# State products two at a time, two batches' scores turned by TensorE, four products in plain fp32

## The chip, the cores and the metric

The kernel runs on one core of one Trainium2 chip. The metric is the device time of one execution in microseconds, as the median of several runs. A profiled execution gives the trace from which the rows below are read.

## The reference

Per batch b (8) and head (8), with x of 512 rows, a state of 32 rows and D = 64, two attentions are computed, and their rows go through a two-layer MLP with softplus:

```python
scores = scale * np.matmul(x, state.transpose(0, 1, 3, 2))
a = np.exp(scores - scores.max(-1, keepdims=True))
a /= a.sum(-1, keepdims=True) + 1e-09
xread = np.matmul(a, state)
scores2 = scale * np.matmul(state, x.transpose(0, 1, 3, 2))
a2 = np.exp(scores2 - scores2.max(-1, keepdims=True))
a2 /= a2.sum(-1, keepdims=True) + 1e-09
sread = np.matmul(a2, x)
attn = np.concatenate([xread, sread], axis=2)
# heads side by side: rows of 512
h = rows @ w_in                      # 4608 x 512 x 2048
g = np.maximum(h, 0.0) + np.log1p(np.exp(-np.abs(h)))
out = g @ w_out                      # 4608 x 2048 x 512
```

The weights come in double precision; the output is fp32.

## The kernel before

**The algebra.** xread is not formed. For each batch b and each chunk c of 512 columns of w_in the kernel forms the *state product* V = state @ w_in of each head (`heads`, L308), and the first layer is then h = V^T a, a product over 256 pairs of head and state row instead of 512 model columns. The second half, 256 rows of sread, is carried to the end as "batch 8".

**Precision.** Operands of the big products are split into a high and a low part in fp32r (`split`, L232: a cast `vh`, `ah`, `gh`, `wh` on ScalarE, then a subtraction `vl`, `al`, `gl`, `wl`), and each product runs as three passes (`PASSES`). An MLP product h.b.f (128 of the 2048 columns, 512 rows) is six matmuls of 512 columns, `gemm1` at L468; each of the four m.b.f.c that follow it adds it into one of four accumulators with three matmuls. A state product V.b.c has eight small plain-fp32 products, each of which uses 64 rows and 32 columns of the array (`heads`, L308); it fills two PSUM banks, and the trace shows two instructions for each plain-fp32 product. Scores Q.b have the same form. The read R.b uses 32 columns of the array for each product. G.b.g and T.b are transposes by TensorE (four blocks, and one).

**Softmax of a batch** (`softmax`, L337), for each half g of the heads: A transposes the scores in 32 by 32 blocks on VectorE, M takes the maximum, Ms subtracts, m is the exponential on ScalarE, N the reciprocal sum, Nm multiplies (VectorE or GpSimd), D transposes back into `af`, and ah/al split it. For the sread side, qk copies the scores to SBUF, E and e make the row softmax, G turns it, R multiplies with x, X scales, T turns and th/tl split.

**Weights.** A slice of w_in or w_out is loaded by SP (Li, Lo) and converted by ch (ScalarE), cu and cr (VectorE). The first chunk of w_in comes in four pieces (two halves j of the columns, two halves x of the heads), and the state products of the first chunk of batches 0 and 1 are issued in halves, V.b.0.j.x, as the pieces arrive.

**The order** is written out by hand: `PLAN` is a list of `name:engine:places`, S for SP's loads and stores, T TensorE, V VectorE, A ScalarE, G GpSimd; places are PSUM banks (0 to 7) or SBUF slots. Each engine works through its own entries in that order; an instruction that waits holds up all that stand behind it on its engine. Fillers w.i (two transposes of the identity) stand in TensorE's list where it would have nothing to do at the start. `TURNS` gives the turns in which batches 0 and 1 alternate; from batch 2 on a batch runs from f = 0 to 15.

Of the kernel before, what the change touches and what calls it, by code (L numbers as in the profile page):

```python
# [18 lines left out]
P = 128  # L19
# [9 lines left out]
WARMERS = 60  # L29
PAIRS = ("w8", "o8", "x", "xT", "po", "wf", "W", "V", "a", "g", "u")  # L30

PLAN = """
Lt.0.0:S:0 Lz.0:S:0 Lt.0.1:S:1 Li.0.1:S:2 Lt.1.0:S:3 w.6:T:0 Q.0:T:1,2 Li.0.2:S:4 qk.0.1:A:2 A.0.1:V:1 w.11:T:3 Lz.1:S:3 A.0.0:V:4 ch.0.1:A:5
Lt.1.1:S:5 M.0.1:V: Li.0.0:S:6 qk.0.0:A:6 Lo.1:S:7 cu.0.1:V:8 w.16:T:4 Li.0.3:S:9 M.0.0:V: Ms.0.1:G: w.18:T:5 E.0.0:V: Ms.0.0:G: m.0.1:A: w.21:T:6
e.0.0:A: N.0.1:V: m.0.0:A: G.0.0:T:7 cu.0.2:V:10 ch.0.2:A:7 w.25:T:0 N.0.0:V: Nm.0.1:G: Q.1:T:3,2 D.0.1:V:8 Nm.0.0:G: w.30:T:1 A.1.1:V:9 ch.0.0:A:10
D.0.0:V:11 cr.0.2:V: ah.0.0:A:11 cu.0.0:V: ch.o1:A:12 V.0.0.1.0:T:4,5 M.1.1:V: ah.0.1:A:12 w.39:T:6 cr.0.0:V: Lo.0:S:13 w.40:T:0 ch.0.3:A:13 w.41:T:1
cu.0.3:V: Lo.2:S:14 V.0.0.0.0:T: cr.0.1:V: Lo.5:S:15 w.43:T:6 al.0.0:V: w.44:T:0 V.0.0.0.1:T: al.0.1:V: vh.0.0.0.0:A:16 vh.0.0.1.0:A:17 cr.0.3:V:
vl.0.0.0.0:V: V.0.0.1.1:T: vl.0.0.1.0:V: w.50:T:1 Ms.1.1:V: ch.o0:A:14 Lx.0.0:S:18 h.0.0:T:6 Lx.0.1:S:19 vh.0.0.0.1:A: cu.o0:V:6 m.1.1:A: cu.o1:V:1
Lo.3:S:20 vl.0.0.0.1:V: vh.0.0.1.1:A: h.0.1:T:0 cr.o0:V: ch.o2:A:4 vl.0.0.1.1:V: cr.o1:V: h.0.2:T:1 cu.o2:V:10 A.1.0:V:5 s.0.0:A:7 wh.0:A:21 cr.o2:V:
V.1.0.0.0:T:4,5 gh.0.0:A:22 V.1.0.0.1:T: wl.0:V: s.0.1:A:11 h.0.3:T:6 gl.0.0:V: wh.1:A:23 M.1.0:V: gh.0.1:A:24 m.0.0.1:T:0 wl.1:V: s.0.2:A:8 wh.2:A:25  # L40
V.1.0.1.0:T: gl.0.1:V: gh.0.2:A:26 m.0.0.0:T:1 wl.2:V: s.0.3:A:13 m.0.1.1:T: gl.0.2:V: ga.0.0:A:14 m.0.1.0:T: Ms.1.0:V: gh.0.3:A:27 cu.o3:V:4
qk.1.0:A:12 Li.3.2:S:28 m.0.2.1:T: gl.0.3:V: Lo.6:S:29 m.0.2.0:T: Lo.4:S:30 r.0.0:V: N.1.1:V: Lx.1.0:S:31 m.0.0.2:T:6 m.1.0:A: m.0.1.2:T: E.0.1:V:
# [148 lines left out]
def width(buf):  # L191

    kind = buf.split(".")[0]
    if kind in ("vp", "sc", "gp", "rp", "tp", "h", "acc", "wp"):
        return 0
    return 2 if kind in PAIRS else 1
# [7 lines left out]
def graph(io, at, nc):  # L204
# [89 lines left out]
    W1 = {}  # L294
# [351 lines left out]
```

## Time and profile before

| what | us |
|---|---|
| median of 3 runs (663.84 to 665.02) | 664.52 |
| profiled execution | 664.04 |
| its span | 662.0 |
| TensorE (PE) busy | 650.3 |
| ScalarE (ACT) busy | 341.3 |
| VectorE (DVE) busy | 287.0 |
| GpSimd (POOL) busy | 5.0 |

The span runs from the first to the last recorded instruction of the profiled execution. In a timeline row the first number is the start and the second how long the merged group lasted until its last end; matmuls overlap, so what an item costs on PE is read from its start to the start of the next item. The names say what is written and read: `h<-a,V` is an MLP product, `acc<-W,g` an m product, `vp<-wf,zf` a state product, `sc<-xT,zf` scores, `rp<-x,aT` the read, `gp<-ident,e` a transpose G, `tp` T, `wp` a filler.

### The profile page before, as it was taken

How to read it: one execution, taken by the hardware profiler on the slowest of the kernel's cores; microseconds unless marked ns; L12 is line 12 of the kernel's file. 1: busy time of each engine (PE TensorE's matmuls, PEld its weight loads, DVE VectorE, ACT ScalarE, POOL GpSimd, SP SyncE). 2: the span in 40 equal slices, each digit the busy share in tenths (PEclk: the TensorE clock that was granted, in tenths of full speed). 3: DMA queues.
4: the chain of work that ended last, by engine and by line, in shares of the span. 5: the costliest groups of instructions: out<-in, count | busy, mean ns of one | idle time of the engine just before them, and what ended most of it. 6: DMA issues, size and time to landing. Idle time of an engine off the chain costs nothing.

```text
span 662.0 us, 9405 instructions
## 1 busy us (share of the span) xinstructions
PE 650.3 (98%) x3898; PEld 501.7 (76%) x3898; DVE 287.0 (43%) x540; ACT 341.3 (52%) x583; POOL 5.0 (1%) x10
## 2 busy tenths in 40 slices
PE   6899999999999999999999999999999999999997
PEld 4477777776788878777778777777777788887776
DVE  4898865764542241228212552228213456122220
ACT  3689975754562465337433564337434747243232
POOL 2000000000000000000000000000000000000000
PEclk9899999999999999999999999999999999999999
DMA  8954113300300005000400104000420001000001
GB/s 319 419 200 159 45 51 104 136 1 33 102 26 17 17 32 167 1 33 32 136 1 1 64 6 130 1 33 32 136 64 1 0 2 65 0 21 13 0 1 64
DMA packets 15914, 44.11 MB, mean 67 GB/s; under 512 B 1792, under 2 KB 2816, under 8 KB 15872
## 3 DMA queue, kind: packets, MB, share of 16 engines
q1 hardware_dynamic: 15872, 43.52, 18.8%
q8 instruction: 30, 0.49, 0.3%
q14 instruction: 12, 0.10, 0.0%
HBM read 34.60 MB, written 8.91 MB: 66 GB/s over the span
## 4 chain that ended last, share of the span: by engine, by line
PE 97%; DVE 1%; DMA 1%; ACT 0%; issue 0%; POOL 0%
PE acc L239 56%; PE h L239 30%; PE vp L239 5%; PE sc L239 1%; PE rp L239 1%; PE gp L384 1%; PE h_idle L576 1%; DMA w<-in_w_in_dram 1%; PE wp L446 0%; DVE T L343 0%; DVE wf L286 0%; POOL T L346 0%; PE tp L429 0%; ACT e L373 0%; ACT e L404 0%
## 5 line engine op out<-in xcount | busy, mean ns | idle before, releaser
L239 PE MATMUL acc<-W,g 128*128 128x512 f32 x1632 | 396.7, 392 | 0.0
L239 PEld LDWEIGHTS acc<-W,g 128*128 128x128 f32 x1632 | 303.3, 188 | 75.3 <-issue 11.3
L236 DVE TENSOR_TENSOR g<-t,g 128x512 fp32r<-128x512 f32 x136 | 93.0, 689 | 257.5 <-ACT g L220 257.4
L239 PE MATMUL h<-a,V 128*128 128x512 f32 x768 | 195.5, 394 | 0.0
L453 ACT ACTIVATE t<-h 128x512 f32<-128x512 f32 x136 | 80.7, 599 | 202.6 <-PE h L239 201.9
L239 PEld LDWEIGHTS h<-a,V 128*128 128x128 f32 x768 | 141.9, 188 | 44.4 <-issue 10.1
L220 ACT CAST g<-t 128x512 fp32r<-128x512 f32 x136 | 83.4, 621 | 5.0 <-issue 2.1
L236 DVE TENSOR_TENSOR V<-vp,V 128x512 fp32r<-128x512 f32 (+1 forms) x66 | 42.0, 670 | 46.6 <-ACT V L220 45.7
L220 ACT CAST V<-vp 128x512 fp32r<-128x512 f32 (+1 forms) x66 | 35.2, 577 | 49.3 <-PE vp L239 46.5
L239 PE MATMUL vp<-wf,zf 64*32 64x512 f32 (+1 forms) x544 | 37.8, 582 | 2.8 <-DVE wf L286 1.8
L239 PEld LDWEIGHTS h<-sreadT,u 128*128 128x128 f32 x192 | 24.3, 189 | 1.6 <-issue 0.8
L239 PE MATMUL h<-sreadT,u 128*128 128x256 f32 x192 | 24.7, 284 | 0.0
L453 ACT ACT_TABLE_LOAD x18 | 23.1, 1283 | 1.7 <-PE h L239 1.4
L220 ACT COPY o<-acc 128x512 f32<-128x512 f32 x26 | 14.4, 586 | 10.0 <-PE acc L239 9.4
L239 PEld LDWEIGHTS vp<-wf,zf 64*32 64x32 f32 x544 | 6.8, 105 | 16.0 <-issue 10.7
L343 DVE STREAM_TRANSPOSE T<-sc 128x512 f32<-128x512 f32 x16 | 10.8, 701 | 11.6 <-ACT e L404 10.7
L220 ACT CAST a<-af 128x512 fp32r<-128x512 f32 x16 | 9.8, 622 | 9.9 <-DVE af L357 9.9
L404 ACT COPY e<-sc 128x512 f32<-128x512 f32 x16 | 9.0, 588 | 10.9 <-PE sc L239 10.2
L384 PE MATMUL gp<-ident,e 128*128 128x128 f32 x64 | 9.5, 280 | 4.2 <-ACT e L373 4.2
L220 ACT CAST W<-ow 128x512 fp32r<-128x512 f32 x16 | 10.0, 624 | 6.4 <-PE acc L239 3.5
L350 DVE TENSOR_REDUCE sm<-T 128x16 f32<-128x512 f32 x16 | 10.7, 668 | 5.3 <-ACT T L347 5.3
L236 DVE TENSOR_TENSOR a<-af,a 128x512 fp32r<-128x512 f32 x16 | 10.7, 684 | 5.0 <-ACT a L220 5.0
(61 smaller groups left out, 296.8 us busy)
## 6 DMA issues: line engine op xcount, KB each, us to landing
xT<-in_xt_dram SPq DMA_DIRECT2D x16, 512.0 KB, 5.1
w<-in_w_in_dram SPq DMA_DIRECT2D x16, 512.0 KB, 8.1
o<-in_w_out_dram SPq DMA_DIRECT2D x16, 512.0 KB, 9.4
x<-in_xn_dram SPq DMA_DIRECT2D x16, 512.0 KB, 3.3
out_dram<-o SPq DMA_DIRECT2D x24, 256.0 KB, 2.1
out_dram<-po SPq DMA_DIRECT2D x8, 256.0 KB, 2.7
zf<-in_zp_dram SPq DMA_DIRECT2D x8, 128.0 KB, 5.4
out_dram<-o SPq DMA_DIRECT2D x8, 64.0 KB, 1.7
```

The lines of the kernel that those rows point to most:

```text
L220: nc.scalar.copy(dst, src)
L236: lambda e: eng(e).tensor_tensor(r(dlo()), src(), dhi(), ALU.subtract))
L239: nc.tensor.matmul(dst, lhs, rhs, start=start, stop=stop)
L343: op(f"A.{b}.{g}", "V", tok, [f"{T}:1"], lambda e: nc.vector.transpose(at(T), at(sc)))
L350: nc.vector.tensor_reduce(at(sm), t3(), AX.X, ALU.add)
L384: nc.tensor.transpose(at(f"gp.{b}.{g}")[:, P * c:P * c + P], at(src)[:, P * c:P * c + P], at("ident"))
L404: op(f"qk.{k}", "A", [sc], [f"{ex}:s"], lambda e, sc=sc, ex=ex: nc.scalar.copy(at(ex), at(sc)))
L453: lambda e: nc.scalar.activation(at(f"t.{k}"), at(f"h.{k}"), AF.Softplus))
L576: nc.tensor.matmul(at("h.idle")[:, 0:P], idle, idle, start=True, stop=True)
```

## The change

- **Pairs.** `STATES` lists the state products that are issued together: chunk c of batches 0 and 1 for c = 1 to 3, chunks 0 and 1, and 2 and 3, of each later batch. A pair is sixteen small products in a row, into four PSUM banks. V.1.0 is one full product; V.0.0 keeps its four halves.
- **Scores of batches 0 and 1** (`TURNED`): A and D are transposes by TensorE with the identity, four blocks of 128 by 128 each, into PSUM banks `st` and `ab`; M and Ms read the bank. For batch 0, ac copies the bank to `af`.
- **First four MLP products of batch 0** (h.0.0 to h.0.3): two plain-fp32 products each, from `Vf` (a copy vf of V.0.0) and `af`, in place of six fp32r passes; V.0.0 is not split, and ah.0/al.0 are made later, for the products from f = 4 on.
- **Order and places** are new for the whole table. There are 4 fillers in place of 13. Some copies and conversions have another engine or form (ga on VectorE four times in place of one, cu in its two-step form 13 times in place of 8, ch as Copy 13 times in place of 8, Ms on VectorE always, Nm on GpSimd once in place of twice). The loads at the start come as xT.0 (both), zf.0, xT.1 (both), then w_in pieces 0.0, 0.2, 0.3, zf.1, piece 0.1; before, pieces 0.1, 0.2, 0.0 and 0.3 stood fourth, sixth, ninth and eleventh.

```diff
+TURNED = (0, 1)
+STATES = [((0, c), (1, c)) if c else ((1, 0),) for c in range(4)] + [((b, c), (b, c + 1)) for b in range(2, B) for c in (0, 2)]
...
-vl.0.0.0.0:V: V.0.0.1.1:T: vl.0.0.1.0:V: w.50:T:1 Ms.1.1:V: ch.o0:A:14 Lx.0.0:S:18 h.0.0:T:6 Lx.0.1:S:19 vh.0.0.0.1:A: cu.o0:V:6 m.1.1:A: cu.o1:V:1
+V.1.0:T:5,1 vf.0.0:A: Ms.1.1:V:7 vf.1.0:A: ch.o1:A:9 cr.o0:V: h.0.0:T:2 m.1.1:A: M.1.0:V: wh.0:A:18 N.1.1:V: vh.1.0.0:A:19 h.0.1:T:3 Lo.4:S:20
...
+    for j in range(2):
+        for x in range(2):
+            op(f"V.0.0.{j}.{x}", "T", ["zf.0", W1[0, j, x]], [f"vp.0.0.{g}:{j}{x}" for g in range(2)],
+               lambda e, j=j, x=x: heads(0, 0, (2 * x, 2 * x + 1), slice(256 * j, 256 * j + 256)))
+        for g in range(2):
+            cs = slice(256 * j, 256 * j + 256)
+            op(f"vf.{g}.{j}", "AV", [f"vp.0.0.{g}:{j}{x}" for x in range(2)], [f"Vf.{g}:{j}"],
+               lambda e, g=g, cs=cs: copy(e, at(f"Vf.{g}")[:, cs], at(f"vp.0.0.{g}")[:, cs]))
...
-                op(f"V.{b}.{c}", "T", [f"zf.{b}"] + ins, [f"{v}:" for v in vp], lambda e, b=b, c=c: heads(b, c, range(4), slice(0, 512)))
...
+    for group in STATES:
...
+        def products(e, group=group):
+            for b, c in group:
+                heads(b, c, range(4), slice(0, 512))
+
+        op("V." + "+".join(f"{b}.{c}" for b, c in group), "T", ins, [f"vp.{b}.{c}.{g}:" for b, c in group for g in range(2)], products)
+
+
+    def turned(name, bank, src, tok):
+        def f(e):
+            for c in range(4):
+                nc.tensor.transpose(at(bank)[:, P * c:P * c + P], at(src)[:, P * c:P * c + P], at("ident"))
+
+        op(name, "T", tok, [bank], f)
...
-        op(f"A.{b}.{g}", "V", tok, [f"{T}:1"], lambda e: nc.vector.transpose(at(T), at(sc)))
...
+        if onPE:
+            turned(f"A.{k}", f"st.{k}", ex, [f"{ex}:s"])
+        else:
+            op(f"A.{k}", "V", [sc], [f"{T}:1"], lambda e: nc.vector.transpose(at(T), at(sc)))
+        src, raw = (f"st.{k}", f"st.{k}") if onPE else (T, f"{T}:1")
...
-        op(f"D.{b}.{g}", "V", [f"{T}:4"], [f"af.{b}.{g}"], lambda e: nc.vector.transpose(at(f"af.{b}.{g}"), at(T)))
...
+        if onPE:
+            turned(f"D.{k}", af, T, [f"{T}:4"])
+        else:
+            op(f"D.{k}", "V", [f"{T}:4"], [af], lambda e: nc.vector.transpose(at(af), at(T)))
+        if b == 0:
+            op(f"ac.{k}", "AV", [af], [f"af.{k}"], lambda e: copy(e, at(f"af.{k}"), at(f"ab.{k}")))
+            af = f"af.{k}"
...
-        op(f"e.{b}.{g}", "A", tok + [nm], [out, f"{rs}:1"],
+        op(f"e.{b}.{g}", "A", tok + [nm, f"mx.{b}.{g}"], [out, f"{rs}:1"],
...
+                early = b == 0 and f < 4
...
+                        if early:
+                            mm(at(f"h.{k}"), at(f"Vf.{g}")[:, cs], at(f"af.{b}.{g}"), g == 0, g == 1)
+                        for vi, ai in PASSES if not early else ():
                             mm(at(f"h.{k}"), r(page(f"V.{b}.{f // 4}.{g}", 2, 512)[:, vi, cs]), r(page(f"a.{b}.{g}", 2, S)[:, ai]), n == 0, n == 5)
```

TensorE's list in batch 6, around the state product of its third chunk (`vp_2`; `tp` is T.6, `h_7` the product h.6.7; the second number in `vp_2_0` is the half g), before:

```order
L429 MATMUL tp_4221<-ident,sr_4207 128x128
L239 MATMUL vp_2_0_4223<-wf_0_680,zf_3641 32x512
L239 MATMUL vp_2_1_4224<-wf_0_680,zf_3641 32x512
...
L239 MATMUL vp_2_0_4223<-wf_1_657,zf_3641 32x512
L239 MATMUL vp_2_1_4224<-wf_1_657,zf_3641 32x512
...
L239 MATMUL h_7_4235<-a_0_3920,V_1_0_4070 128x512 x3
```

The same place on TensorE after:

```order
L239 MATMUL acc_0_0_4030<-W_633,g_4_4090 128x512 x3
L239 MATMUL vp_2_0_4190<-wf_0_747,zf_3652 32x512
L239 MATMUL vp_2_1_4191<-wf_0_747,zf_3652 32x512
...
L239 MATMUL vp_3_0_4192<-wf_0_1097,zf_3652 32x512
L239 MATMUL vp_3_1_4193<-wf_0_1097,zf_3652 32x512
...
L239 MATMUL acc_0_1_4036<-W_633,g_4_4090 128x512 x3
L239 MATMUL acc_0_2_4042<-W_633,g_4_4090 128x512 x3
L239 MATMUL acc_0_3_4047<-W_633,g_4_4090 128x512 x3
L444 MATMUL tp_4234<-ident,sr_4184 128x128
L239 MATMUL h_7_4236<-a_0_3906,V_1_0_3927 128x512 x3
```

The fourth chunk (`vp_3`), which stood by itself some products later, now follows the third at once, among the m products of f = 4 (`acc`), and T.6 comes after it.

TensorE's list at the start, from the fillers behind Q.0 to the first MLP product `h_0`, before:

```order
L446 MATMUL wp_155<-ident 128x128 x2
L384 MATMUL gp_0_163<-ident,e_0_0_135 128x128 x4
L446 MATMUL wp_172<-ident 128x128 x2
L239 MATMUL sc_0_179<-xT_0_100,zf_124 32x512
...
L446 MATMUL wp_192<-ident 128x128 x2
L239 MATMUL vp_0_0_207<-wf_0_168,zf_94 32x256
...
L446 MATMUL wp_263<-ident 128x128 x2
L239 MATMUL h_0_271<-a_0_202,V_0_0_252 128x512 x3
```

The same stretch on TensorE after (`st` is written by A, `ab` by D, `vp_0_0_272` by V.1.0):

```order
L344 MATMUL gp_1_147<-ident,e_0_1_119 128x128 x4
L461 MATMUL wp_165<-ident 128x128 x2
L344 MATMUL ab_1_174<-ident,T_1_142 128x128 x4
L461 MATMUL wp_182<-ident 128x128 x2
L239 MATMUL sc_0_188<-xT_0_103,zf_123 32x512
...
L344 MATMUL st_1_232<-ident,e_1_1_215 128x128 x4
L344 MATMUL ab_0_244<-ident,T_0_152 128x128 x4
L344 MATMUL st_0_251<-ident,e_1_0_229 128x128 x4
...
L239 MATMUL vp_0_0_272<-wf_0_163,zf_123 32x512
...
L239 MATMUL h_0_289<-af_0_265,Vf_239 128x512
```

The scores Q.1 now stand behind the transpose D.0.1, and A.1.1, D.0.0, A.1.0 and the whole of V.1.0 stand ahead of the first MLP product, where fillers stood.

## Rows read from the trace of the kernel before

**Rows 1.** The page, busy time of each engine: us, share of span, instructions.

```profile
PE 650.3 (98%) x3898; PEld 501.7 (76%) x3898; DVE 287.0 (43%) x540; ACT 341.3 (52%) x583; POOL 5.0 (1%) x10
```

**Rows 2.** Table by stretch: from:to, length, busy (instructions) of each engine, PEclk, DMA share, GB/s.

```profile
0.00:25.52 25.52, 17.53 (x118) 10.44 (x119) 13.44 (x28) 9.70 (x18) 4.96 (x10) 0.87 0.93 354
14.00:17.40 3.40, 3.40 (x24) 1.37 (x23) 2.41 (x7) 1.44 (x3) 2.10 (x2) 0.50 1.03 412
20.80:24.20 3.40, 3.02 (x20) 1.00 (x20) 2.62 (x5) 0.42 (x3) 0.00 (x0) 0.50 1.03 418
27.60:150.00 122.40, 122.14 (x759) 92.42 (x758) 93.12 (x185) 94.26 (x155) 0.00 (x0) 1.00 0.32 113
```

**Rows 3.** Timeline of PE around V.4.1: start, us until its last end, item.

```profile
324.40 2.88 PE L239 MATMUL acc<-W,g 128*128 128x512 f32 x12
327.21 1.09 PE L239 MATMUL vp<-wf,zf 64*32 64x512 f32 x16
328.23 1.65 PE L239 MATMUL h<-a,V 128*128 128x512 f32 x6
329.72 2.90 PE L239 MATMUL acc<-W,g 128*128 128x512 f32 x12
```

**Rows 4.** Timeline of PE around V.0.3 and V.2.2, which stand together.

```profile
152.85 0.84 PE L239 MATMUL acc<-W,g 128*128 128x512 f32 x3
153.62 1.95 PE L239 MATMUL vp<-wf,zf 64*32 64x512 f32 x32
155.50 3.69 PE L239 MATMUL acc<-W,g 128*128 128x512 f32 x15
159.12 1.09 PE L239 MATMUL sc<-xT,zf 64*32 64x512 f32 x16
```

**Rows 5.** The page's groups: busy us, mean ns | idle before, releaser.

```profile
L236 DVE TENSOR_TENSOR V<-vp,V 128x512 fp32r<-128x512 f32 (+1 forms) x66 | 42.0, 670 | 46.6 <-ACT V L220 45.7
L220 ACT CAST V<-vp 128x512 fp32r<-128x512 f32 (+1 forms) x66 | 35.2, 577 | 49.3 <-PE vp L239 46.5
```

**Rows 6.** Timeline of PE from the first MLP product on.

```profile
25.52 4.36 PE L239 MATMUL h<-a,V 128*128 128x512 f32 x18
29.81 0.66 PE L239 MATMUL vp<-wf,zf 64*32 64x256 f32 x16
30.40 1.65 PE L239 MATMUL h<-a,V 128*128 128x512 f32 x6
...
32.68 0.64 PE L239 MATMUL vp<-wf,zf 64*32 64x256 f32 x8
33.25 6.41 PE L239 MATMUL acc<-W,g 128*128 128x512 f32 x27
```

**Rows 7.** Timeline of PE in batch 4: two transposes, and the read.

```profile
338.59 1.03 PE L384 MATMUL gp<-ident,e 128*128 128x128 f32 x8
339.38 2.30 PE L239 MATMUL acc<-W,g 128*128 128x512 f32 x9
...
342.97 1.10 PE L239 MATMUL rp<-x,aT 128*32 128x64 f32 x64
344.00 3.02 PE L239 MATMUL acc<-W,g 128*128 128x512 f32 x12
```

**Rows 8.** Timeline of PE, the idle products at the very start.

```profile
1.05 5.49 PE L576 MATMUL h_idle<-idle 128*128 128x128 f32 x24 [1.05 <-DVE idle L574]
```

**Rows 9.** Timeline of PE and POOL at the start: G.0.0, Nm.0.1, filler, Q.1, filler.

```profile
13.83 1.00 PE L384 MATMUL gp<-ident,e 128*128 128x128 f32 x4 [4.22 <-ACT e L373]
14.43 1.05 POOL L356 TENSOR_TENSOR T<-T,sm 128x512 f32<-128x512 f32 x1 [1.03 <-ACT T L347]
14.63 0.63 PE L446 MATMUL wp<-ident 128*128 128x128 f32 x2
15.19 1.96 PE L239 MATMUL sc<-xT,zf 64*32 64x512 f32 x16
17.08 0.57 PE L446 MATMUL wp<-ident 128*128 128x128 f32 x2
```

More of the change, by code (lines that the diff above doesn't have):

```diff
@@ L39 @@
[L39 to L42, printed above, removed]
@@ L193, in width @@
     kind = buf.split(".")[0]
-    if kind in ("vp", "sc", "gp", "rp", "tp", "h", "acc", "wp"):
+    if kind in ("vp", "sc", "gp", "st", "ab", "rp", "tp", "h", "acc", "wp"):
         return 0
@@ L315, in graph @@
     for b in range(B):
         for c in range(4):
-            halves = b < 2 and c == 0
-            vp = [f"vp.{b}.{c}.{g}" for g in range(2)]
-            if halves:
-                for j in range(2):
-                    for x in range(2):
-                        op(f"V.{b}.{c}.{j}.{x}", "T", [f"zf.{b}", W1[0, j, x]], [f"{v}:{j}{x}" for v in vp],
-                           lambda e, b=b, j=j, x=x: heads(b, 0, (2 * x, 2 * x + 1), slice(256 * j, 256 * j + 256)))
-            else:
-                ins = [W1[0, j, x] for j in range(2) for x in range(2)] if c == 0 else [W1[c, q] for q in range(4)]
-                op(f"V.{b}.{c}", "T", [f"zf.{b}"] + ins, [f"{v}:" for v in vp], lambda e, b=b, c=c: heads(b, c, range(4), slice(0, 512)))
@@ L327, in graph @@
-            for g in range(2):
-                for j in range(2) if halves and b == 0 else (None,):
-                    k = f"{b}.{c}.{g}" + ("" if j is None else f".{j}")
-                    cs = slice(0, 512) if j is None else slice(256 * j, 256 * j + 256)
-                    ins = [f"{vp[g]}:"] if not halves else [f"{vp[g]}:{y}{x}" for y in ((0, 1) if j is None else (j,)) for x in range(2)]
-                    V = f"V.{b}.{c}.{g}"
-                    split(f"vh.{k}", f"vl.{k}", lambda g=g, cs=cs, vp=vp: at(vp[g])[:, cs], lambda V=V, cs=cs: page(V, 2, 512)[:, 0, cs],
-                          lambda V=V, cs=cs: page(V, 2, 512)[:, 1, cs], ins, f"{V}:h{j}", f"{V}:l{j}", "A")
@@ L337, in softmax @@
-    def softmax(b, g, sc, tok):
-        T = f"T.{b}.{g}"
-        t3 = lambda: page(T, 16, NS)
-        wide = lambda ap: ap.unsqueeze(2).broadcast_to([P, 16, NS])
-        mx, sm = f"mx.{b}.{g}", f"sm.{b}.{g}"
-        op(f"A.{b}.{g}", "V", tok, [f"{T}:1"], lambda e: nc.vector.transpose(at(T), at(sc)))
-        op(f"M.{b}.{g}", "V", [f"{T}:1"], [mx], lambda e: nc.vector.tensor_reduce(at(mx), t3(), AX.X, ALU.max))
-        op(f"Ms.{b}.{g}", "VG", [f"{T}:1", mx], [f"{T}:2"],
-           lambda e: eng(e).tensor_tensor(t3(), t3(), wide(at(mx)), ALU.subtract))
-        op(f"m.{b}.{g}", "A", [f"{T}:2"], [f"{T}:3"], lambda e: nc.scalar.activation(at(T), at(T), AF.Exp, scale=SCALE))
+            for g in range(2) if (b, c) != (0, 0) else ():
+                k = f"{b}.{c}.{g}"
+                split(f"vh.{k}", f"vl.{k}", lambda k=k: at(f"vp.{k}"), lambda k=k: page(f"V.{k}", 2, 512)[:, 0],
+                      lambda k=k: page(f"V.{k}", 2, 512)[:, 1], [f"vp.{k}:"], f"V.{k}:h", f"V.{k}:l", "A")
@@ new lines, in graph @@
+    for group in STATES:
+        ins = [f"zf.{b}" for b in dict.fromkeys(b for b, c in group)]
+        for c in dict.fromkeys(c for b, c in group):
+            ins += [W1[0, j, x] for j in range(2) for x in range(2)] if c == 0 else [W1[c, q] for q in range(4)]
+        def products(e, group=group):
+            for b, c in group:
+                heads(b, c, range(4), slice(0, 512))
+        op("V." + "+".join(f"{b}.{c}" for b, c in group), "T", ins, [f"vp.{b}.{c}.{g}:" for b, c in group for g in range(2)], products)
@@ L379, in rowexp @@
         op(f"r.{b}.{g}", "V", [f"{rs}:1"], [f"{rs}:2"], f)
-    def turned(b, g, src, tok):
-        def f(e):
-            for c in range(4):
-                nc.tensor.transpose(at(f"gp.{b}.{g}")[:, P * c:P * c + P], at(src)[:, P * c:P * c + P], at("ident"))
-        op(f"G.{b}.{g}", "T", tok, [f"gp.{b}.{g}"], f)
     for b in range(B):
```

303 lines of the change are left out of this document (158 added, 145 removed).

## The prediction, made before the changed kernel ran

> **What bounds the kernel now.** I read the page's line of engines first: TensorE is busy for 98% of the span [rows 1]. Then the table by stretch: up to the first MLP product, at 25.52 us, PE is busy 17.53 us; from 27.6 to 150 us, the stage with the most other work, it is busy 122.14 of 122.40 us while VectorE and ScalarE have about a quarter of their time free [rows 2]. So behind 25.5 us the end is set by how much PE has to do. A change there is priced by PE's start-to-start times, not by busy times, because consecutive matmuls overlap. Ahead of 25.5 us PE waits for the softmax and the weights, and the bound is a chain through all engines.
>
> In the dense stage the times are very regular. Twelve fp32r products of 512 columns would take 12 x 0.227 = 2.72 us; six take 1.36 us (an h product, three m products being 0.68 us). What is over that lies around the work that uses a part of the array. In [rows 3] the twelve products ahead of a state product take 327.21 - 324.40 = 2.81 us (0.09 over), the state product 1.02 us, and the six products behind it 1.49 us (0.13 over). A lone state product of one batch and chunk thus costs 0.09 + 1.02 + 0.13 = **1.24 us** of PE. At 153.62 us two of them stand next to each other, by chance: 153.62 to 155.50 is 1.88 us, three products ahead of it take 0.77 us instead of 0.68, and the fifteen behind it carry the 0.13 of leaving and the 0.09 of the next entry (3.62 us, 3.40 by count) [rows 4]. Two together cost 0.09 + 1.88 + 0.13 = **2.10 us**, not 2.48: the second adds 0.86 us.
>
> **The change part by part.**
>
> *State products in pairs.* Before, 30 full state products stand in PE's list after the first MLP product, 28 with no other next to them and two together: 28 x 1.24 + 2.10 = 36.8 us. After, there are 15 pairs: 15 x 2.10 = 31.5 us. That is **-5.3 us**. Each pair fills four PSUM banks where a single fills two; the casts (0.58 us each on ScalarE) and subtractions (0.67 us each on VectorE) that empty them [rows 5] are as many as before, and hidden as long as the next user of those banks comes later. In the order of batch 6 three m products (2.04 us), the transpose of the read and the next h product follow the pair, and the casts of the first half can begin 0.86 us before the second half ends; I cost it at nothing, and price the failure as a rival.
>
> *The first chunk of batch 1.* Its half products stood between MLP products: 0.59, 0.57 and (as the other two) 0.57 us with an entry and exit of 0.22 us around two of them [rows 6]: 2.2 us behind the first h. They are now one product, ahead of the first h. **-2.2 us** behind 25.5 us; what it costs ahead of it stands under the start.
>
> *Neighbours.* The new order puts R.0, R.1, the pair V.0.3+1.3 and Q.2 in one row, and joins R.2 and Q.3 to pairs; before, Q.2 with R.1 and V.2.1 with R.2 were joined. That is three junctions more without the 0.22 us of leaving and entering, and at two of them (a state product followed by scores of the same shape) the 0.16 us by which the second of two was cheaper as well: 3 x 0.22 + 2 x 0.16, about **-1.0 us**. R itself, 342.97 to 344.00 us, costs 1.03 us between [rows 7], the same on both sides.
>
> *Scores of batches 0 and 1 transposed by PE.* Eight transposes of four blocks come onto PE and eight stream transposes leave VectorE. Two, D.1.0 and D.1.1, stand behind the first h. The nearest rows are two such groups in a row: 338.59 to 339.38 us, with about 0.1 us at the exit [rows 7]: **+0.9 us**. The other six stand ahead of it. The extra copies (two of 512 columns, four of 256 in place of four casts) lie on ScalarE beside PE's list; late ones would cost their own length. The Trainium skill speaks against this move: "VectorE: DVE Perf Modes", under "Rules for kernel authors", has the DVE's transpose as the fastest for blocks of 32 by 32 within a bank, and that is all this kernel needed. By that rule the exchange is a loss of engine time; by the rows it is 0.9 us of the bounding engine, and what it buys is in the chain at the start only.
>
> *First four MLP products in plain fp32.* Six fp32r products (1.36 us) become two fp32 products each. No row has a dense fp32 product of 512 columns. Below, nothing: 0. Above, the idle products at the start, 128 columns of plain fp32, 12 of them (24 instructions) in 5.49 us [rows 8]: 0.457 us each, four times that for 512 columns is 1.83 us, so 8 x (1.83 - 0.68) = +9.2 us. Nearest is the second state product of [rows 4]: 512 columns of the same number type at 2.4 GHz, 0.86 us. I take it: 8 x (0.86 - 0.68) = **+1.4 us**.
>
> *The start.* The first h comes at 25.52 us [rows 6]. With the change PE's list up to it is: D.0.1, a filler, Q.1, three half products of batch 0, three transposes, the last half, V.1.0, then h. D.0.1 needs the multiplication on GpSimd that ends at 14.43 + 1.05 = 15.5 us [rows 9]; I leave it there although the subtraction before it moves to VectorE. From 13.83 to 15.19 us one group of transposes and a filler took 1.36 us, and Q.1 1.9 us more, both at the low clock [rows 9]: Q.1 ends at 18.8 us. Then three halves of which two run side by side (2 x 0.57), three transposes (3 x 0.36, half of the pair in [rows 7]), a half (0.3) and V.1.0 (1.02) make 3.5 us: h at 22.3 us with PE at 2.4 GHz, 25.8 us with PE at 1.2 GHz. The granted clock was 0.50 in two stretches of this start, 14.0 to 17.4 and 20.8 to 24.2 us [rows 2]; the first followed on 4.2 us without work on PE, ahead of 13.83 us [rows 9]. I expect one such stretch, not two, since behind D.0.1 the new list leaves PE no long wait, and add 1 us because ScalarE must cast for these products in turn: 23.5 us, **-2.0 us**, between -3.2 and +0.3. The slices of w_in that the first chunk needs are loads 6, 7, 8 and 10 in SP's list (4, 6, 9 and 11 before); the other loads keep their number, and I cost SP's new order at nothing: with the transfers running ahead of their use by several us, a late one would stop PE for what it is late.
>
> *Other moves* (casts and copies between ScalarE and VectorE, fewer fillers, two table loads fewer on ScalarE) lie on engines with time to spare [rows 2]; the last products, copies and stores have the same form.
>
> **The sum.** -5.3 - 2.2 - 1.0 + 0.9 + 1.4 - 2.0 = -8.2 us. The profiled execution took 664.04 us for a span of 662.0; the median of the runs is 664.52. Less 8.2 the profiled one gives 655.8, the median 656.3 us. I forecast **656.3**. With the bounds of the start and of the fp32 products at 0, the case lies between 653.7 (1.4 + 1.2 less) and 658.6 (start at +0.3).
>
> **The rivals.**
>
> *Pairs don't overlap.* If the second half of a pair begins only after the first has drained, a pair saves one entry and exit (0.22 us) and no more: 15 x 0.22 = 3.3 in place of 5.3 us, and the neighbours lose 0.3: **658.6 us**. Against it: [rows 4], though that is one pair, and of two batches. The Trainium skill ("TensorEngine Tiling (Array Packing)", Key Properties) has it that a change of tiling mode drains the engine and a change of tile doesn't; [rows 3, 4] agree, with 0.22 us at the borders.
>
> *The start stays cold.* With fewer fillers and a wait for D.0.1 PE may be at 1.2 GHz until the first products and through some of them: h at 25.8 us, and the first 3.4 us of products doubled, 1.7 us: -8.2 + 2.3 + 1.7: **660.3 us**. For it: two cold stretches in this trace with 13 fillers, now 4.
>
> *The start is better.* h at 22.3 us and fp32 products at no extra cost: **653.7 us**.
>
> *Four banks at once.* PE stops behind every pair because casts come too late to free the banks: VectorE needs four subtractions of 0.67 us behind the first cast, 0.58 + 4 x 0.67 = 3.3 us, against 2.0 us of m products; a wait of up to 1.2 us, 15 times, is +18 us, **674 us**, slower. It decides from 0.55 us per pair on. For it: ScalarE at 77% in the crowded stretch [rows 2]. In sentences of its own: the Trainium skill's tiling page, under "PSUM Bottleneck", warns that tiling speeds up TensorE and not the emptying of PSUM; by it the 18 us are real. Against it: not all four banks are wanted next, and PE waited hardly at all in this stage, with the same number of casts.
>
> **How the numbers follow.** Forecast (654.5 to 658): 0.48. Better start 0.20, no overlap 0.10, cold start 0.14, four banks 0.05. The far end of the fp32 products, +9.2 us, would give 664.1, no change: 0.03. The range leaves out the last two and the tails: 653.0 to 660.5. A measurement of this kernel tells 0.2%, 1.3 us, from no change. Faster holds in all cases but these two: faster 0.92, same 0.03, slower 0.05.
>
> **What would show it.** In the profile after: state products as rows of 32 instructions about 1.9 us from the next row, with 0.1 us over count at each border; the first h between 22.3 and 25.8 us; four products of fp32 with about 1.7 us from one to the next; no wait of PE behind pairs; PE busy about 8 us less in sum. The forecast is wrong if PE shows waits of more than 0.5 us behind pairs, if the first h comes after 26 us, or if plain fp32 streams far slower than 0.86 us.

## The result, and the profile after

The changed kernel takes **653.92 us** (median of 4 runs, 652.99 to 654.01) beside 664.76 us for the kernel before on the same chip: a ratio of 0.9836, 95% interval 0.9819 to 0.9853. The forecast was 656.3 us in a range from 653.0 to 660.5. The profiled execution took 654.01 us, with a span of 652.0 us beside 662.0. So the gain is 10.8 us by the medians and 10.0 us between the two profiled executions; the forecast had 8.2.

The page's line of engines, which answers to [rows 1] (TensorE's time fell by 8.4 us and is still 98% of the span):

```profile
PE 641.9 (98%) x3888; PEld 504.0 (77%) x3888; DVE 286.3 (44%) x538; ACT 336.0 (52%) x581; POOL 1.7 (0%) x7
```

TensorE's timeline from the first transposes to the second group of m products, beside [rows 6, 9]:

```profile
8.55 1.15 PE L344 MATMUL st<-ident,e 128*128 128x128 f32 x8 [0.73 <-ACT e L419]
...
14.33 0.65 PE L344 MATMUL ab<-ident,T 128*128 128x128 f32 x4 [3.07 <-POOL T L371]
...
15.23 1.96 PE L239 MATMUL sc<-xT,zf 64*32 64x512 f32 x16
16.94 1.76 PE L239 MATMUL vp<-wf,zf 64*32 64x256 f32 x24
...
21.51 7.13 PE L239 MATMUL h<-af,Vf 128*128 128x512 f32 x16
28.08 8.75 PE L239 MATMUL acc<-W,g 128*128 128x512 f32 x36
36.67 1.03 PE L344 MATMUL ab<-ident,T 128*128 128x128 f32 x8
37.46 2.98 PE L239 MATMUL acc<-W,g 128*128 128x512 f32 x12
40.28 2.88 PE L239 MATMUL h<-a,V 128*128 128x512 f32 x12
```

The first MLP product comes at 21.51 us: **4.0 us** earlier than the 25.52 us before. Behind it lie 652.0 - 21.51 = 630.5 us of span, beside 662.0 - 25.52 = 636.5: **6.0 us** less. The forecast had 2.0 and 6.2.

The table by stretch (columns as in [rows 2]): one stretch of lowered clock where there were two (a granted clock of 0.50, that is 1.2 GHz, from about 15.0 to 18.4 us, which the first two rows share, hence their means of 0.64 and 0.85), and TensorE almost without a pause:

```profile
14.00:17.40 3.40, 3.07 (x34) 1.52 (x42) 3.37 (x9) 1.26 (x3) 0.28 (x1) 0.64 1.03 419
17.40:20.80 3.40, 3.40 (x56) 2.08 (x44) 2.72 (x6) 3.18 (x8) 0.00 (x0) 0.85 1.04 418
20.80:24.20 3.40, 3.40 (x19) 1.26 (x8) 3.27 (x8) 3.38 (x7) 0.00 (x0) 1.00 1.02 417
```

A pair that stands by itself, on TensorE's timeline, beside [rows 3, 4]:

```profile
300.15 2.20 PE L239 MATMUL acc<-W,g 128*128 128x512 f32 x9
302.28 1.95 PE L239 MATMUL vp<-wf,zf 64*32 64x512 f32 x32
304.16 2.33 PE L239 MATMUL acc<-W,g 128*128 128x512 f32 x9
306.33 1.52 PE L239 MATMUL h<-a,V 128*128 128x512 f32 x6
```

Nine products ahead take 2.13 us (2.04 by count), the pair 1.88, nine behind it 2.17: 0.09 + 1.88 + 0.13 = 2.10 us, the figure of the forecast.

### The profile page after: what moved, and what is told of

The parts are those of the page before. It is cut to its first block, busy times and chain, and to the rows that moved or that the text cites. A ratio compares the mean times of both kernels' runs of the same rounds, so it can differ in the third digit from the quotient of the medians.

```text
span 652.0 us, 9421 instructions
## 1 busy us (share of the span) xinstructions
PE 641.9 (98%) x3888; PEld 504.0 (77%) x3888; DVE 286.3 (44%) x538; ACT 336.0 (52%) x581; POOL 1.7 (0%) x7
## 4 chain that ended last, share of the span: by engine, by line
PE 96%; DMA 2%; DVE 1%; ACT 0%; issue 0%; POOLq 0%; SPq 0%; DVEq 0%
PE acc L239 57%; PE h L239 31%; PE vp L239 4%; PE sc L239 1%; PE gp L344 1%; PE rp L239 1%; DMA o<-in_w_out_dram 1%; DMA zf<-in_zp_dram 1%; PE ab L344 0%; DVE mx L359 0%; DVE nm L387 0%; DVE V L236 0%; POOLq L655 0%; PE st L344 0%; SPq L227 0%
## 5 line engine op out<-in xcount | busy, mean ns | idle before, releaser
L239 PE MATMUL h<-a,V 128*128 128x512 f32 x744 | 188.0, 391 | 0.4 <-DVE V L236 0.4
L220 ACT CAST g<-t 128x512 fp32r<-128x512 f32 x136 | 82.8, 620 | 10.8 <-PE acc L239 7.8
L236 DVE TENSOR_TENSOR V<-vp,V 128x512 fp32r<-128x512 f32 x62 | 39.4, 682 | 11.1 <-ACT V L220 10.9
L220 ACT CAST V<-vp 128x512 fp32r<-128x512 f32 x62 | 32.8, 596 | 13.2 <-PE vp L239 13.2
L239 PE MATMUL vp<-wf,zf 64*32 64x512 f32 (+1 forms) x528 | 32.5, 592 | 0.0
L387 DVE TENSOR_REDUCE nm<-e 128x1 f32<-128x512 f32 x16 | 10.8, 675 | 13.7 <-ACT e L419 13.7
L236 DVE TENSOR_TENSOR u<-wf,u 128x512 fp32r<-128x512 f32 x16 | 10.4, 687 | 7.7 <-ACT u L220 7.7
L362 ACT ACTIVATE T<-T 128x512 f32<-128x512 f32 x16 | 10.0, 631 | 6.7 <-DVE T L361 6.6
L286 DVE SCALAR_TENSOR_TENSOR ow<-h_o,ow 128x512 int32<-128x512 int32 x16 | 11.0, 686 | 5.4 <-ACT h_o L271 3.5
L395 ACT ACTIVATE e<-e,nm 128x512 f32<-128x512 f32 x16 | 11.6, 726 | 1.2 <-DVE nm L388 1.2
L286 DVE SCALAR_TENSOR_TENSOR wf<-h,wf 128x512 int32<-128x512 int32 x16 | 10.7, 686 | 2.8 <-ACT h L271 2.7
```

The source lines that it names most:

```text
L220: nc.scalar.copy(dst, src)
L236: lambda e: eng(e).tensor_tensor(r(dlo()), src(), dhi(), ALU.subtract))
L239: nc.tensor.matmul(dst, lhs, rhs, start=start, stop=stop)
L286: nc.vector.scalar_tensor_tensor(u, h2().bitcast(I32), 3, u, ALU.logical_shift_left, ALU.bitwise_or)
L362: op(f"m.{k}", "A", [f"{T}:2"], [f"{T}:3"], lambda e: nc.scalar.activation(at(T), at(T), AF.Exp, scale=SCALE))
L387: nc.vector.tensor_reduce(at(nm), at(sc), AX.X, ALU.max)
```

## The experiments

All are the changed kernel, unedited (after_again, after_third) or with one to four edits. Times are medians; "before" is the kernel before on the same chip in the same session, and medians of different sessions are compared by their ratios; the first MLP product and the span are of the profiled execution, and "rest" is the span less the first.

| run | us | before | ratio (95%) | span | first h | rest |
|---|---|---|---|---|---|---|
| changed kernel | 653.92 | 664.76 | 0.9836 (0.9819 to 0.9853) | 652.0 | 21.51 | 630.5 |
| after_again | 653.13 | 665.57 | 0.9814 (0.9795 to 0.9834) | 651.0 | 20.41 | 630.6 |
| e1_singles | 658.23 | 665.57 | 0.9884 (0.9864 to 0.9903) | 655.0 | 21.34 | 633.7 |
| e4_q1_first | 654.01 | 665.57 | 0.9822 (0.9804 to 0.984) | 651.3 | 22.33 | 629.0 |
| e5_a0_dve | 655.02 | 665.57 | 0.9834 (0.9815 to 0.9853) | 653.2 | 23.84 | 629.4 |
| e2_onepass | 654.07 | 666.62 | 0.9818 (0.9793 to 0.9843) | 650.6 | 21.36 | 629.2 |
| e3_fillers | 652.28 | 666.62 | 0.9791 (0.9764 to 0.9818) | 650.5 | 20.47 | 630.0 |
| after_third | 654.51 | 664.72 | 0.9849 (0.9828 to 0.9871) | 650.8 | 21.36 | 629.4 |
| e6_o12_later | 653.84 | 664.72 | 0.9836 (0.9817 to 0.9856) | 652.0 | 23.01 | 629.0 |
| e7_fill_o12 | 652.02 | 664.72 | 0.9807 (0.9788 to 0.9826) | 650.0 | 20.57 | 629.4 |
| e8_q1_in_wait | 651.71 | 664.72 | 0.9803 (0.9784 to 0.9822) | 649.6 | 20.37 | 629.2 |

### The changed kernel once more

> The changed kernel once more, on the chip of the runs beside it, so that their differences are taken on one chip. All theories: 653.9 us, first MLP product at 21.5 us, 626.2 us from there to the last instruction of TensorE.

This execution shows what the start is worth without the lowered clock. TensorE's timeline, and one line of the table by stretch:

```profile
14.23 0.66 PE L344 MATMUL ab<-ident,T 128*128 128x128 f32 x4 [3.06 <-POOL T L371]
...
15.03 1.09 PE L239 MATMUL sc<-xT,zf 64*32 64x512 f32 x16
15.92 1.68 PE L239 MATMUL vp<-wf,zf 64*32 64x256 f32 x24
17.53 0.66 PE L344 MATMUL st<-ident,e 128*128 128x128 f32 x4
...
18.98 1.49 PE L239 MATMUL vp<-wf,zf 64*32 64x256 f32 x24
20.41 7.13 PE L239 MATMUL h<-af,Vf 128*128 128x512 f32 x16
```

```profile
14.00:17.40 3.40, 3.17 (x46) 1.38 (x46) 3.37 (x9) 2.35 (x5) 0.17 (x1) 1.00 1.04 422
```

The granted clock is 1.00 where it was 0.64, Q.1 takes 0.89 us instead of 1.71, and the first h product comes 1.1 us sooner, although D.0.1 starts within 0.1 us of the first profile. So the same kernel has starts that differ by a microsecond.

### Pairs taken apart

> Twelve of the fifteen pairs are split: the second state product stands behind the next h product or group of m products. The three pairs that stand in a row with R or Q stay adjacent. Theory (a border costs 0.22 us, and the second of two adjacent products costs 0.86 instead of 1.02 us): each split pair costs 2 x 1.24 - 2.10 = 0.38 us more, 12 x 0.38 = +4.6 us behind the first h product, 658.5 us; the start stays at 21.5 us. Rival 1 (products of a pair don't overlap, only the border is saved): 12 x 0.22 = +2.6 us, 656.5 us. Rival 2 (the gain behind the first h product comes from the new order, not from the pairs): no change, 653.9 us.

```diff
-STATES = [((0, c), (1, c)) if c else ((1, 0),) for c in range(4)] + [((b, c), (b, c + 1)) for b in range(2, B) for c in (0, 2)]
+STATES = [((b, c),) for b in range(B) for c in range(4) if (b, c) != (0, 0)]
...
-V.0.1+1.1:T:0,3,5,4
+V.0.1:T:0,3
...
+V.1.1:T:5,4
```

TensorE's timeline in batch 4:

```profile
338.22 1.09 PE L241 MATMUL vp<-wf,zf 64*32 64x512 f32 x16
339.24 0.96 PE L241 MATMUL acc<-W,g 128*128 128x512 f32 x3
340.13 1.09 PE L241 MATMUL vp<-wf,zf 64*32 64x512 f32 x16
341.15 1.66 PE L241 MATMUL acc<-W,g 128*128 128x512 f32 x6
```

Each half costs its full 1.02 us again, and the m product between them 0.89 us for 0.68. Behind the first h product this kernel takes 633.7 us. It does not wait there; the runs of the changed kernel's form that do not wait there either, e4 and e6, take 629.0. The difference, 4.7 us, is the 4.6 of the theory: the products of a pair do run into each other, and both rivals fall. The medians differ by 5.1 us.

### The four products in one pass

> The first four MLP products of batch 0 are one fp32r pass each, two instructions of 512 columns per product instead of two plain-fp32 products: the low parts of V.0.0 and of batch 0's weights a are left out in these four. Theory (plain fp32 costs 0.86 us for 512 columns and TensorE is the bound there): 8 x (0.86 - 0.227) = -5.1 us, 648.8 us. Rival (the first m product behind them waits for softplus and subtraction of h.0.0, whose gl ends at 27.2 us in the changed kernel, while TensorE starts that m product at 28.08): only about 0.9 us are gained, 653.0 us, and TensorE waits some 4 us ahead of the first m product. In the second case the four products in plain fp32 cost almost nothing that fp32r passes would not also have cost.

```diff
...
-                            mm(at(f"h.{k}"), at(f"Vf.{g}")[:, cs], at(f"af.{b}.{g}"), g == 0, g == 1)
+                            mm(at(f"h.{k}"), r(at(f"Vf.{g}")[:, cs]), r(at(f"af.{b}.{g}")), g == 0, g == 1)
```

The copies into `Vf` and `af` write fp32r here. TensorE:

```profile
21.36 2.11 PE L241 MATMUL h<-af,Vf 128*128 128x512 f32 x8
26.38 9.63 PE L241 MATMUL acc<-W,g 128*128 128x512 f32 x36 [2.91 <-ACT g L222]
35.87 1.09 PE L346 MATMUL ab<-ident,T 128*128 128x128 f32 x8
```

TensorE does the four products in about 2 us and then stands still until ScalarE has made g. From the first h product to D.1.0 this kernel takes 35.87 - 21.36 = 14.51 us, the changed one 36.67 - 21.51 = 15.16: only **0.65 us** of the 5.1 are gained. The rival is right: TensorE now waits 2.91 us for ScalarE ahead of the first m product. ScalarE (busy 3.38 of 3.40 us in the changed kernel's row from 20.80 us) gives the pace, and plain fp32 fills time that TensorE would have waited. The low parts of these four products are left out in this run; the six-pass form, with the splits that it needs, was not run in this place.

### Fillers ahead of D.0.1

> Ten more fillers (two transposes of the identity each) stand in TensorE's list ahead of the transpose D.0.1, in the 3.07 us in which TensorE waits for GpSimd. Theory (the granted clock of 0.5 from 14.98 to 18.40 us follows on that wait): the clock stays at 1.0 through that stretch, Q.1 and the half products take about half as long, first h product 1 to 1.7 us earlier, 652.2 to 652.9 us. Rival (the clock falls all the same, or the stretch waits for other engines): 653.9 us, first h product at 21.5 us.

```diff
-w.25:T:7
+w.25:T:7 w.26:T:1 w.27:T:2 w.28:T:5 w.29:T:0 w.31:T:7 w.32:T:1 w.33:T:2 w.34:T:5 w.35:T:0 w.36:T:7
```

```profile
10.84 2.57 PE L463 MATMUL wp<-ident 128*128 128x128 f32 x22
14.28 0.66 PE L346 MATMUL ab<-ident,T 128*128 128x128 f32 x4 [0.88 <-POOL T L373]
...
20.47 7.13 PE L241 MATMUL h<-af,Vf 128*128 128x512 f32 x16
```

The mean granted clock is 1.000 in all five executions; the changed kernel has 1.000 in one execution of 13 over its three sessions, and 0.994 to 0.997 in the others. The first h product is 1.0 us earlier than in the first profile, as the theory has it. Beside the ten fillers D.0.1 starts no later, at 14.28 us, so they cost nothing here. In time the run is at the fast end: its ratio of 0.9791 is below the 0.9814 to 0.9849 of the changed kernel's three sessions, but its interval overlaps with that of after_again.

### Q.1 moved ahead

> One entry of TensorE's list is moved: the scores Q.1 stand ahead of the transpose D.0.1, for which TensorE waits 3.07 us, instead of behind it. Theory (the start is bound by TensorE's list behind D.0.1): the 1.71 us of Q.1 vanish from between D.0.1 and the first h product, less what ScalarE's copies then make TensorE wait; first h product at about 20.5 us, 652.9 us. Rival (the first h product waits for ScalarE's copies or for the pieces of w_in, whatever TensorE does before): first h product at 21.5 us, 653.9 us.

```diff
-D.0.1:T:0 cu.0.2:V: Lo.0:S:9 w.30:T:2 cr.0.0:V: ac.0.1:A:8 Q.1:T:1,5
+Q.1:T:1,5 D.0.1:T:0 cu.0.2:V: Lo.0:S:9 w.30:T:2 cr.0.0:V: ac.0.1:A:8
```

```profile
14.29 1.59 PE L241 MATMUL sc<-xT,zf 64*32 64x512 f32 x16 [3.00 <-issue]
15.81 1.11 PE L346 MATMUL ab<-ident,T 128*128 128x128 f32 x4
...
22.33 7.13 PE L241 MATMUL h<-af,Vf 128*128 128x512 f32 x16
```

Neither theory: Q.1 did not run in the wait, it waited itself, until 14.29 us, and held up D.0.1 by 1.5 us. The timeline names no releaser, but its operand zf.1 is the ninth load, behind three pieces of w_in, and this is its issue on SP:

```profile
4.79 0.52 SPq L229 DMA_DIRECT2D zf<-in_zp_dram  x1
```

It landed 9.4 us after its issue, so at 14.2 us, just ahead of Q.1. In e8, where zf.1 is loaded ahead of the pieces of w_in, it is issued at 3.16 us, lands 6.4 us later, and Q.1 has no such wait.

### A of batch 0 back on VectorE

> The two transposes A.0.1 and A.0.0 of batch 0's scores go back to VectorE; D.0.1, D.0.0 and batch 1 stay on TensorE. Theory (the start begins with the chain of batch 0's softmax, and A on TensorE brought D.0.1 forward, which the prediction left at 15.5 us): D.0.1 starts at about 15.5 instead of 14.33 us, the first h product at about 22.6, 655.0 us. Rival 1 (D.0.1 came earlier because the idle products and Q.0 at the very start were done sooner, whoever makes A): D.0.1 at 14.3 us, first h product at 21.5, 653.9 us. Rival 2 (weights or ScalarE set the first h product): D.0.1 later, but the first h product at 21.5, 653.9 us.

```diff
-A.0.1:T:3 A.0.0:T:4
+A.0.1:V:4 A.0.0:V:5
...
-        if onPE:
+        if b == 1:
             turned(f"A.{k}", f"st.{k}", ex, [f"{ex}:s"])
...
```

A in blocks of 32 by 32 and D in blocks of 128 by 128 are not each other's inverse, so batch 0's weights lie in other places here and the output is not the reference's; the instructions and their shapes are what they would be. VectorE, TensorE, and two lines of the table by stretch:

```profile
9.38 1.30 DVE L359 STREAM_TRANSPOSE T<-sc 128x512 f32<-128x512 f32 x2
10.61 1.24 DVE L361 TENSOR_REDUCE mx<-T 128x16 f32<-128x512 f32 x2
```

```profile
15.58 1.12 PE L346 MATMUL ab<-ident,T 128*128 128x128 f32 x4 [4.20 <-POOL T L373]
...
23.84 7.13 PE L241 MATMUL h<-af,Vf 128*128 128x512 f32 x16
```

```profile
14.00:17.40 3.40, 1.82 (x14) 1.37 (x22) 3.30 (x10) 1.50 (x4) 1.05 (x1) 0.50 1.04 424
17.40:20.80 3.40, 3.40 (x41) 1.15 (x26) 2.35 (x5) 2.14 (x4) 0.00 (x0) 0.50 1.03 420
```

The two transposes cost VectorE 1.23 us in the middle of its chain, and D.0.1 starts 1.25 us later, at the 15.5 us which the prediction had kept. The subtractions stay on VectorE in this run, so their move away from GpSimd does not by itself bring D.0.1 forward. On TensorE the two transposes take 0.98 us (8.55 to 9.53 us), while it has nothing else to do. The first h product is later by more than the theory's 1.1 us, by 2.3: TensorE's wait ahead of D.0.1 is 4.20 instead of 3.07 us, and the granted clock is 0.50 through both stretches (it fell earlier, at about 11.1 us: the stretch from 10.20 to 13.60 us has 0.63). Rivals 1 and 2 fall.

### A wait at 122 us

Leaving e1 aside, the rest of the runs differs by up to 1.6 us, and the longest belong to two executions of the changed kernel. TensorE and VectorE of after_again around 122 us:

```profile
119.37 1.06 PE L239 MATMUL sc<-xT,zf 64*32 64x512 f32 x16
...
124.15 1.66 PE L239 MATMUL acc<-W,g 128*128 128x512 f32 x6 [0.29 <-DVE T L357]
126.19 1.62 PE L239 MATMUL h<-a,V 128*128 128x512 f32 x6 [0.38 <-DVE V L236]
127.65 2.22 PE L239 MATMUL acc<-W,g 128*128 128x512 f32 x9
```

```profile
122.09 0.49 DVE L281 TENSOR_SCALAR ow<-o 128x512 uint16<-128x512 uint16 x1 [2.59 <-DMA o<-in_w_out_dram]
...
122.78 0.70 DVE L236 TENSOR_TENSOR V<-vp,V 128x512 fp32r<-128x512 f32 x1
123.37 0.72 DVE L357 STREAM_TRANSPOSE T<-sc 128x512 f32<-128x512 f32 x1
```

VectorE waits 2.59 us for a slice of w_out, o12, and the subtractions of the pair V.0.3+1.3 and the transpose A.2.0 stand behind it, for which TensorE waits in turn. In the first profile VectorE's wait is 2.54 us. When o12 is loaded (SP), in the kernel before and in after_again, and its first conversion cu.o12 in the kernel before:

```profile
117.83 0.80 SPq L227 DMA_DIRECT2D o<-in_w_out_dram  x2
```

```profile
115.80 1.30 SPq L227 DMA_DIRECT2D o<-in_w_out_dram  x3
```

```profile
127.02 0.40 DVE L281 TENSOR_SCALAR ow<-o 128x512 uint16<-128x512 uint16 x1
```

Before, o12 is the second of its two loads, issued at 118.25 us, and VectorE comes to it 8.8 us later, without a wait. In after_again it is the first of three, issued at 115.80 us, and VectorE comes to it at 119.50 us, 3.7 us after the issue. The load was not issued later; the new order has cu.o12 ahead of the subtractions of V.0.3+1.3 and of A.2.0 in VectorE's list, where it stood behind A.2.0, M.2.0 and N.2.1 before.

> The changed kernel once more, on the chip of the three runs beside it. 653 to 654 us; first MLP product at 20.4 us where the granted clock is 1.0 through the start, at 21.5 us where it is 0.5 from about 15 to 18.4 us; TensorE waits about 1.2 us in sum between 123 and 128 us in the first case.

Here VectorE waits 1.51 us, with the first h product at 21.36 us, and the rest is 629.4 us. The issue of o12 moves with the start; what differs is how long the transfer takes. From issue to cu.o12 it is 6.2 us in the first profile, 6.3 in after_again, 5.2 here, and 4.6 and 4.7 in e1 and e5, where TensorE does not wait there.

> One entry of VectorE's list is moved: cu.o12, the first conversion of the w_out slice o12, stands behind the subtraction vl.0.3.1 instead of ahead of the subtractions and of A.2.0 that follow the pair V.0.3+1.3. Theory (VectorE waits there for the transfer of o12, 2.6 us in the repeated run of the changed kernel, and TensorE's T.0, m.1.8.2 and h.0.13 wait for what is queued behind it): the waits of TensorE between 123 and 128 us, 0.9 to 1.2 us in sum, vanish, and the time is 0.7 to 1.2 us less than that of the changed kernel beside it. Rival (TensorE waits there for the subtractions themselves, or for ScalarE's casts ahead of them): the waits stay, no change.

```diff
-cu.o12:W:1 Lx.2.1:S:0 vh.0.3.0:A:17 m.1.8.1:T:3 vl.1.3.0:V:
+Lx.2.1:S:0 vh.0.3.0:A:17 m.1.8.1:T:3 vl.1.3.0:V:
...
-vl.0.3.1:V: m.1.9.2:T:
+vl.0.3.1:V: cu.o12:W:1 m.1.9.2:T:
```

The same place in e6:

```profile
121.96 1.06 PE L241 MATMUL sc<-xT,zf 64*32 64x512 f32 x16
...
128.69 1.52 PE L241 MATMUL acc<-W,g 128*128 128x512 f32 x6
```

From Q.2 to the end of the h product h.0.13 TensorE takes 128.69 - 121.96 = 6.73 us, in after_again 127.65 - 119.37 = 8.28: **1.55 us** are lost there. But e6 also had the latest start of the runs with A on TensorE (its idle products took 5.49 us, beside 4.69 in the first profile, D.0.1 came at 14.73, and the granted clock was 0.50 from 14.0 to 17.4 us), so by itself it doesn't tell the moved entry from a late start: in e4 and e5, with cu.o12 in its old place and late starts, TensorE doesn't wait there either. Its median is 0.7 us below that of the run beside it, the lower end of what was expected, and the intervals of the two ratios overlap. e7 tells them apart, with an early start and the moved entry:

> Both edits: the ten fillers ahead of D.0.1 and cu.o12 behind vl.0.3.1. Theory (the fillers keep the clock at 1.0, which brings the first MLP product to 20.4 us, and part of that was given back in the wait for o12): 2 us less than the changed kernel beside it, about 651.5 us, and no wait of TensorE behind the first MLP product. Rival (the start's gain is given back in another place behind it): no less than the changed kernel with fillers alone, which was 1.8 us ahead of the one-pass kernel beside it.

Its first h product is at 20.57 us, and TensorE has no wait behind it; the rest is 629.4 us, beside 630.6 for after_again at the same start. The median is 2.5 us below that of the changed kernel beside it. So the wait is the slice's: at an early start it is there with cu.o12 in its old place (after_again, and 0.38 us of TensorE in e3) and gone with cu.o12 moved. What the moved entry gives by itself in time is not shown: e7's ratio of 0.9807 is not below the 0.9791 of the fillers alone, and the rival is refused by the trace only.

> The kernel with both edits, and besides zf.1 loaded ahead of the four pieces of w_in and Q.1 ahead of D.0.1, so that Q.1 runs in TensorE's wait for GpSimd. Theory 1 (Q.1 stood in TensorE's wait for zf.1 when only Q.1 was moved; behind D.0.1 TensorE's list is the bound): the 0.89 us of Q.1 leave the path, first MLP product at about 19.5 us, 0.9 us less than the kernel with both edits. Theory 2 (behind D.0.1 the half products wait for VectorE's conversions of the w_in pieces, on which VectorE is busy all the time): first MLP product at 20.4 us, no change, and TensorE waits for VectorE ahead of the half products.

```diff
-Li.0.0:S:4 Li.0.2:S:5 qk.0.1:A:1 Li.0.3:S:6 Lz.1:S:2
+Lz.1:S:2 Li.0.0:S:4 Li.0.2:S:5 qk.0.1:A:1 Li.0.3:S:6
...
```

The other edits are those of e7 and e4. TensorE's timeline:

```profile
13.23 1.09 PE L241 MATMUL sc<-xT,zf 64*32 64x512 f32 x16
...
15.38 0.64 PE L241 MATMUL vp<-wf,zf 64*32 64x256 f32 x8 [0.25 <-DVE wf L288]
16.32 1.24 PE L241 MATMUL vp<-wf,zf 64*32 64x256 f32 x16 [0.30 <-DVE wf L288]
...
20.37 7.13 PE L241 MATMUL h<-af,Vf 128*128 128x512 f32 x16
```

Q.1 is off the path, and the half products wait for VectorE's conversions of w_in instead: theory 2. The first h product gains 0.2 us of the 0.89, the median 0.3 us, which the intervals do not tell from nothing. This is the version with the lowest median, 651.71 us, 2.8 us below the changed kernel in the same session.

## Why the prediction was right, and where it was not

The gain was forecast as 8.2 us and is 10.0 us between the profiled executions. The time lies in the stated range, but below the part of it that was called likeliest (654.5 to 658 us). The pairs were right in mechanism and price; the start was mis-sized; and the part behind the first h product came out by two errors that cancel.

**Pairs** (-5.3 us): right in price (2.10 us) and in mechanism (e1: 4.7 us for 12 pairs, 4.6 by the same prices). TensorE shows no wait behind a lone pair: the four banks come free in time.

**The start** (-2.0 us, bounds -3.2 and +0.3) is the term that was mis-sized: it gave -4.0, outside its bounds. The failed step is "I leave it there": D.0.1 kept at 15.5 us because GpSimd's multiplication is before it. The chain ahead of that multiplication had become shorter by the two transposes, 1.25 us by e5; D.0.1 came at 14.33. The prediction had said of the move that it buys something "in the chain at the start only", and then gave that chain nothing. Here the Trainium skill's rule ("VectorE: DVE Perf Modes", Rules for kernel authors) has to be read with the place: 1.23 us on the engine that others wait for cost more than 0.98 us on one that is idle.

The rest of that term, step by step: D.0.1 and the filler behind it take 0.90 us instead of the 1.36 read at the low clock, Q.1 1.71 instead of 1.9, and the prediction's own steps add up to 23.3 us, not 23.5. With the 1.2 us of D.0.1 these are the 2.0 us. At a clock of 1.0 Q.1 takes 0.89 us, and the first h product comes at 20.4 us. The 1 us added because ScalarE must cast was right in size by luck: from Q.1's end to the first h product it is 4.5 us beside the 3.5 counted, in after_again too, where the half products take 1.61 us (1.14 counted), the three transposes 1.45 (1.08), the last half and V.1.0 1.43 (1.32). TensorE shows no wait for ScalarE's copies there; the weight loads of the half products wait 1.0 us in sum, and that for VectorE's conversions of w_in.

**Behind the first h product** the sum of -6.2 us met -6.0, but by two errors that cancel. Without a wait there (e4, e6) it is 629.0 - 636.5 = -7.5 us; the wait for o12 takes 1.5 us of that back (120.44 to 128.66 us in the first profile, 8.22 us beside 6.73). The sentence that failed is the one on loads, "with the transfers running ahead of their use by several us". SP's order, which it costs at nothing, is not what changed for o12; VectorE's order is, and it stopped TensorE by way of VectorE's queue. Of the 1.3 us by which the count was short, no experiment here shows the places. The traces show junctions that were not counted: nine groups of transposes G stand alone before and three after, and three transposes T stand right ahead of a state product before (0.20 us to the next start, 0.03 elsewhere).

**The first chunk of batch 1** (-2.2 us) and **the neighbours** (-1.0 us) have no experiment of their own. The traces agree: the changed kernel has no half product behind the first h product, and R.0, R.1, the pair V.0.3+1.3 and Q.2 stand in a row from 116.78 to 121.44 us, in which the pair takes 1.74 us instead of 1.88.

**Four products in fp32** (+1.4 us): the price was right. Their 16 instructions take 28.08 - 21.51 = 6.57 us, and the 36 behind them 36.67 - 28.08 = 8.59 us, 0.43 more than by count, of which 0.09 is the entry of the next transposes: 6.9 us, or 0.86 for each of the eight plain-fp32 products, 1.5 over the six-pass form by count. But it is not what the path pays: one pass in place of plain fp32 gains only 0.65 us (e2), since ScalarE sets the pace there.

**D.1.0 and D.1.1** (+0.9 us): 37.46 - 36.67 = 0.79 us, and twelve products behind them 2.82 us, 0.1 over count: as priced.

**The rivals.** "Pairs don't overlap" and "four banks at once" fell with e1 and the rows of the pair. "The start stays cold" was half there: one stretch, in most executions, which costs 1.1 us (20.41 beside 21.51 us). "The start is better" (653.7 us) is nearest to the result, but the start was better still, and its fp32 half came true for another reason, ScalarE's pace.

## What to carry to other kernels

Small products that use a part of the array are cheapest next to each other: count their borders, not only their own time. Where an operation leaves the chain that others wait for, recompute every start behind it, a fixed time read from the old trace included. And when an engine's list is reordered, an entry that needs a transfer can come up before the transfer has landed: compare its new time with the load's issue, and look at what is queued behind it.

## What the runs showed of the hardware

Of 13 executions of the changed kernel, one had a mean granted clock of 1.000; with fillers in the 3 us ahead of D.0.1, 13 of 13 (e3, e7, e8). Where the clock fell it was to 0.50: in the first profile just behind the wait of 3.07 us ahead of D.0.1, in e6 inside that wait (0.50 from 14.0 us on, D.0.1 at 14.73), in e5 behind a shorter one of 2.18 us. In after_again the same wait of 3.06 us had no such effect. With and without the low stretch the first h product of one kernel came at 21.51 and 20.41 us. The Trainium skill ("TensorE: Matmul & The Clock Gate", Part 1: The HAM clock gate) says that the number of products at the low clock varies from run to run of one kernel; after_again and the first profile agree: no stretch at the low level and one, with D.0.1 at 14.23 and 14.33 us.
